# A gated recurrence followed by a max-out layer: copies that either VectorE or ScalarE may do, and a new order of all queues

## Chip, cores and metric

The kernel runs on one NeuronCore of a Trainium2 chip. The metric is the device time of one execution in microseconds. TensorE is called PE here, VectorE DVE, ScalarE ACT, GpSimd POOL and SyncE SP. Each engine works through its own queue of instructions strictly in the order in which they were written; semaphores make an instruction wait for another engine or for a transfer.

## The reference

```python
# q, k, v, f_logit: (B=4, H=8, S=768, D=48), float32
f = 1 / (1 + exp(-f_logit))
for t in range(S):
    state = f[:, :, t, :, None] * state + einsum('bhd,bhe->bhde', k[:, :, t], v[:, :, t])
    y[:, :, t] = einsum('bhd,bhde->bhe', q[:, :, t], state)

x = y.transpose(0, 2, 1, 3).reshape(B * S, H * D)      # 3072 x 384
h1, h2 = x @ w1, x @ w2                                # 384 x 1024 each
out = maximum(h1, h2) @ w_out                          # 1024 x 384
```

## The kernel before

The sequence is cut into windows of 256 positions, three for each of the four batch entries: twelve stages s = 0 to 11, where stage s is window s // 4 of batch entry s % 4. A partition of the 128 holds two neighbouring positions. Each window consists of two halves h = 0 and 1 of 128 positions, and the state is carried from half to half and, by way of stage s - 4, from window to window.

The kernel writes max(h1, h2) as relu(h1 - h2) + h2. So it needs two matrices made from the weights: `wd` = w1 - w2, and `m2` = w2 @ w_out. The output is xT·m2 + relu(xT·wd)·wo.

What each engine does is written as a list of short words, `ORDER`, and the kernel issues the steps in the order of that list. Since every step writes instructions into several queues, the list fixes the order of all five queues. No scheduler moves anything later. The words are these, with the stage behind the letter:

- `Lf`, `Lk`, `Lq`, `Lv`: load an input of a stage (384 KB) from SP's queue. f has 3 buffers, k and q have 4, v has 6, and a load waits until its buffer is free. It also waits for an earlier transfer, as the transfers of the SP and ACT queues share eight completion semaphores. `W1:i`, `W2:i`: gather 128 rows of a weight (512 KB) from POOL's queue. `Wo:i`: load half of `w_out` from SP's queue.
- `E`: two activations on ACT (exp, then ln) that give -log f in `both`. `e` on POOL or `g` on DVE adds the two positions into `es`.
- `C`: five matmuls on PE for the running sum `cum`; DVE makes `even`. `X`: five exponentials on ACT (`f_inv`, `f_dec`, `f_last`).
- `K` on POOL or `k` on DVE: `kp` = k times `f_inv`. `Q` or `q`: `qp` = q times `f_dec`, likewise. `V` on DVE or `U` on ACT: v in bf16 (`vb`).
- `T`: 32 transposes of `kp` and `qp` on PE (line 236), and two copies of the results, `trs`, on DVE (line 239).
- `A`: the products of keys and queries, 32 matmuls, and four products with a mask on DVE (`at_m`, line 264).
- `D` and `N`: what the window adds to the state (32 matmuls, or 16 where one half is enough), and the new state for half 0 and half 1. Where there is an older state, DVE adds (line 336) and POOL multiplies (line 337).
- `S`: the state's part of y. `Z`: a tiny ACT copy of it. `Y`: the rest of y on PE (line 306), two ACT copies into `xT` (line 344), and two small transfers from ACT's queue that close gaps in `xT` (line 347).
- `d<s>.<i>`: a quarter of relu(xT·wd): six matmuls (line 360) and a relu on ACT (line 362). `o<s>.<i>`: half of the output of stage s: eleven matmuls (lines 370 and 373), a copy on DVE (line 375), and with the second half the store from SP's queue.
- `wc`, `wT`, `wo`, `wm`, `ws`: casts, transposes and products of the weights. The letter behind names the engine that does the cast or copy: a for ACT, v for DVE, p for POOL. `ws` makes half of `wd` (line 405), `wm` a third of `m2` (line 399).

All matrix results go through eight PSUM banks that are handed out in turn, so a new one waits for the reader of the eighth one before.

Of the kernel before, what the change touches and what calls it, by code (L numbers as in the profile page):

```python
# [14 lines left out]


ORDER = """
Lf:0 E0 Lv:0 e0 C0 X0 Lk:0 V0 W2:0 Lf:1 K0 Lq:0 Lv:1 E1 q0 e1 T0 Lk:1 C1 Lf:2 W1:0 Lq:1 A0 X1 wca0
V1 D0 S0 K1 W1:1 W2:1 W2:2 E2 Lf:3 N0 g2 W1:2 Lk:2 Lq:2 q1 D1 Z0 Y0 T1 N1 E3 e3 A1 wTa0 C2 S1 Lv:2
wcp1 C3 Wo:0 Z1 wcv2 Wo:1 Lf:4 X2 wsv0 wsv1 Y1 q2 X3 k2 Lk:3 wTa1 Lv:3 Lq:3 V2 wTv2 d0.0 d0.1 d0.2  # L20
d0.3 Lf:5 T2 wov0 d1.0 d1.1 wov2 Lk:4 d1.2 woa3 A2 Lv:4 D2 d1.3 Lq:4 Lf:6 wop1 E4 wma2 Lk:5 wma0 N2
g4 Q3 k3 wmv1 C4 U3 S2 D3 Z2 N3 Lq:5 X4 o1.0 T3 E5 Y2 e5 o0.0 K4 C5 X5 A3 Lf:7 V4 S3 Q4 o0.1 T4 Z3
Lv:5 E6 Y3 Lf:8 D4 Lq:6 e6 Lk:6 N4 Lv:6 d2.0 o1.1 A4 K5 E7 S4 Z4 d2.1 Lq:7 d2.2 d2.3 Lf:9 Y4 V5 D5
Lv:7 N5 d3.0 d3.1 g7 d3.2 C6 q5 Lf:10 o2.0 X6 K6 Lv:8 C7 X7 T5 o2.1 A5 S5 Lk:7 E8 Z5 e8 d3.3 U6 d4.0
d4.1 C8 Y5 q6 q7 X8 Lk:8 K7 V7 o3.0 Lq:8 T6 d4.2 o3.1 d4.3 E9 E10 D6 e9 N6 A6 d5.0 o4.0 Lv:9 d5.1
d5.2 d5.3 C9 e10 D7 N7 S6 Z6 Lf:11 X9 Lq:9 Lk:9 Lq:10 T7 Y6 Q8 o4.1 U9 Lk:10 A7 K8 V8 S7 o5.0 C10 Z7
k9 E11 Lv:10 Y7 Lv:11 Lq:11 X10 D8 Q9 Lk:11 T8 o5.1 d6.0 d6.1 d6.2 A8 S8 Q10 D9 Z8 d6.3 d7.0 T9 Y8
o6.0 d7.1 K10 d7.2 A9 e11 T10 U10 d7.3 o6.1 C11 o7.0 X11 S9 Z9 D10 K11 A10 Y9 o7.1 d8.0 d8.1 d8.2
V11 Q11 d8.3 S10 T11 Z10 D11 Y10 o8.0 d9.0 o8.1 d9.1 d9.2 d9.3 A11 S11 d10.0 Z11 d10.1 d10.2 Y11
o9.0 d10.3 o9.1 o10.0 d11.0 d11.1 d11.2 d11.3 o10.1 o11.0 o11.1  # L30
"""


# [1 line left out]
def kernel(  # L35
# [20 lines left out]
    nc = tc.nc  # L56
    B, H, S, D = q.shape
# [20 lines left out]
    def bank(name, dtype=F32):  # L78
        return psum.tile([C, 2048 // (4 if dtype == F32 else 2)], dtype, name=name, tag="bank")
# [47 lines left out]
    for nm, n_bufs in (("es", 2), ("kp", 3), ("qp", 2), ("vb", 3)):  # L127
        padded[nm] = []
        for i in range(n_bufs):
            t = consts.tile([C, H, DP] if nm == "es" else [C, 2, H, DP], BF16, name=f"{nm}{i}")  # L130
# [3 lines left out]
    def pad(nm, s):  # L134
        return padded[nm][s % len(padded[nm])]
# [86 lines left out]
    def stage_V(s, copy):  # L222
        copy(pad("vb", s)[:, :, :, 0:D], by_parity(loaded[s]["v"]))

    def stage_T(s):
        t = work.tile([C, 2, 2, NP, 2, HC], BF16, name="trs", tag="trs", bufs=3)
        ps = [bank(f"trp{h}", BF16).rearrange("p (x j a t) -> p x j a t", x=2, j=NP, a=2)
              for h in range(2)]
        for x, nm in enumerate(("kp", "qp")):
            src = pad(nm, s)  # L230
            for j in range(NP):
                for par in range(2):
                    for h in range(2):
                        rows = slice(h * HC, (h + 1) * HC)
                        pair = src[rows, par, 2 * j:2 * j + 2, :].rearrange("p r d -> p (r d)")
                        nc.tensor.transpose(out=ps[h][:, x, j, par, :], in_=pair,  # L236
                                            identity=ident[rows, rows])
        for h in range(2):
            nc.vector.tensor_copy(t[:, h], ps[h])  # L239
        tr[s] = t  # L240

    def stage_A(s):
        t = tr[s]
        m = work.tile([C, 2, NP, 2, C], BF16, name="at_m", tag="at_m")
        for jj in range(2):
            ps = [bank(f"at{r}").rearrange("p (j a t) -> p j a t", j=2, a=2) for r in range(2)]
            for j in range(2 * jj, 2 * jj + 2):
                for par in range(2):
                    for h in range(2):
                        for r in range(2):  # L250
                            rows = slice(r * DP, r * DP + D)
                            nc.tensor.matmul(out=ps[r][h * HC:(h + 1) * HC, j % 2, par, :],  # L252
                                                  lhsT=t[rows, h, 0, j, par, :],
                                                  rhs=t[rows, h, 1, j].rearrange("p a t -> p (a t)"),
                                                  start=True, stop=True, skip_group_check=True)
            at[s, jj] = ps
        at[s] = m

    def stage_A_dve(s):
        m = at[s]  # L260
        for jj in range(2):
            ps = at.pop((s, jj))
            for r in range(2):
                nc.vector.tensor_mul(m[:, r, 2 * jj:2 * jj + 2], ps[r],  # L264
                                     mask.rearrange("p j a b t -> p j a (b t)"))

    ys = {}

    def has_state(s, h):
        return s >= B or h > 0  # L270

    def state_before(s, h):
        return states[s][:, 0] if h else states[s - B][:, 1]
# [22 lines left out]
    def stage_Yv(s):  # L296


        m, vb = at.pop(s), pad("vb", s)
        for j in range(NP):  # L300
            for par in range(2):
                for r in range(2):
                    for h in (1, 0):
                        rows = slice(h * HC, (h + 1) * HC)
                        first = j == 0 and par == 0 and not has_state(s, h)
                        nc.tensor.matmul(  # L306
                            out=ys[s][h][r * DP:(r + 1) * DP, j, :], lhsT=vb[rows, par, 2 * j + r, :],
                            rhs=m[rows, r, j, par, :], start=first,
                            stop=(j == NP - 1 and par == 1), skip_group_check=True)

    def stage_D(s):
        kp, vb = pad("kp", s), pad("vb", s)
        halves = range(2) if s < n_s - B else range(1)
        sadd[s] = [bank(f"sadd{h}")[:, 0:NP * DP].rearrange("p (j e) -> p j e", j=NP) for h in halves]
        for j in range(NP):
            for par in range(2):
                for r in range(2):
                    for h in halves:
                        rows = slice(h * HC, (h + 1) * HC)
                        nc.tensor.matmul(  # L320
                            out=sadd[s][h][r * DP:(r + 1) * DP, j, :], lhsT=kp[rows, par, 2 * j + r, :],
                            rhs=vb[rows, par, 2 * j + r, :], start=(j == 0 and par == 0),
                            stop=(j == NP - 1 and par == 1), skip_group_check=True)
        states[s] = work.tile([C, 2, NP, DP], BF16, name="state", tag=f"state{s % B}")

    def stage_D_dve(s, h):
        if h >= len(sadd[s]):
            return
        ps = sadd[s][h]
        f_last = dec[s][2][:, :, h:h + 1].to_broadcast([C, NP, DP])  # L330
        new = states[s][:, h]
        if not has_state(s, h):
            nc.vector.tensor_mul(new, ps, f_last)  # L333
        else:
            tmp = work.tile([C, NP, DP], F32, name="tmp_s", tag="tmp_s")
            nc.vector.tensor_add(tmp, ps, state_before(s, h))  # L336
            nc.gpsimd.tensor_mul(new, tmp, f_last)  # L337

    xT, gT, obs = {}, {}, {}

    def stage_Y_act(s):
        x = xpool.tile([C, NP, 2, 2, HC], BF16, name="xT", tag="xT", bufs=3)
        for h, ps in enumerate(ys.pop(s)):
            nc.scalar.copy(x[:, :, :, h, :], ps.rearrange("p j (a t) -> p j a t", a=2))  # L344
        x = x.rearrange("p j a h t -> p j (a h t)")
        for r in range(2):
            nc.scalar.dma_start(out=x[r * DP + D:(r + 1) * DP, 0:KT, :],
                                in_=x[r * DP:r * DP + D, KT, :])
        xT[s] = x
        tr.pop(s)  # L350
# [59 lines left out]
    def attention(fn):  # L410
        return lambda a: fn(int(a))
# [4 lines left out]
    def rows_of(dst, w):  # L416
# [8 lines left out]
        "K": lambda a: stage_M(int(a), "k", nc.gpsimd), "k": lambda a: stage_M(int(a), "k", nc.vector),  # L425
        "Q": lambda a: stage_M(int(a), "q", nc.gpsimd), "q": lambda a: stage_M(int(a), "q", nc.vector),
        "V": lambda a: stage_V(int(a), nc.vector.tensor_copy), "U": lambda a: stage_V(int(a), nc.scalar.copy),
        "T": attention(stage_T), "S": attention(stage_S), "Z": attention(stage_Z),
        "A": lambda a: (stage_A(int(a)), stage_A_dve(int(a))),
        "Y": lambda a: (stage_Yv(int(a)), stage_Y_act(int(a))),  # L430
        "D": lambda a: (stage_D(int(a)), stage_D_dve(int(a), 0)),
        "N": lambda a: stage_D_dve(int(a), 1),
        "d": lambda a: piece_d(*map(int, a.split("."))), "o": lambda a: piece_o(*map(int, a.split("."))),
# [37 lines left out]
```

## Time and profile before

| what | us |
|---|---|
| median of 5 runs | 148.35 |
| lowest and highest of them | 147.28 and 149.04 |
| the profiled execution | 148.52 |
| its span, first to last instruction | 146.8 |
| PE busy | 124.2 (85%) |
| DVE busy | 95.9 (65%) |
| ACT busy | 89.8 (61%) |
| POOL busy | 59.3 (40%) |

In a profile, busy time and shares are averages over the span. The rows of digits cut the span into 40 equal slices of 3.67 us; a digit is the busy share of a slice in tenths. A group of instructions has its line, engine, operation, output and input tiles, count, busy time and mean. The chain of work that ended last goes back from the last instruction, at each step to what released it; each of its lines has a start, a length, and what ran. In the timeline an instruction's wait stands in brackets, with what ended it. Matmuls overlap, so a matmul's own length is longer than what it costs the queue; the distances in the chain are the better measure.

### The profile page before, as it was taken

The page shows a single profiled execution, that of the slowest core. Times are in us where ns is not written, and L with a number is a line of the kernel's source. Part 1 is how long each engine was busy: PE and PEld are TensorE (multiplying, and loading weights), DVE is VectorE, ACT ScalarE, POOL GpSimd, SP SyncE. Part 2 cuts the span into 40 slices and gives each one's busy share as a digit, 9 for nine tenths or more (in the row PEclk, how much of TensorE's full clock was granted, in tenths as well). Part 3 has the DMA queues.
Part 4 walks back from the last instruction along what each step waited for, and adds up shares of the span by engine and source line. Part 5 has one row for each costly group of instructions (what it writes and reads, how often), then busy time and mean ns, then how long its engine had stood idle before and what let it go on. Part 6 is the DMA issues. An engine that isn't in the chain of part 4 may idle for free.

```text
span 146.8 us, 5288 instructions
## 1 busy us (share of the span) xinstructions
PE 124.2 (85%) x2292; PEld 91.1 (62%) x2292; DVE 95.9 (65%) x179; ACT 89.8 (61%) x179; POOL 59.3 (40%) x68
## 2 busy tenths in 40 slices
PE   0017378769999999999997999999999999999990
PEld 0005266546866667876865786786767877866750
DVE  5157988489698697877893858958497752613030
ACT  3462947774697886959967886596527634650500
POOL 7376776232019484544214639195404610000000
PEclk9999999999999999999999999999999999999999
DMA  4999999999989706999997985993002300202022
GB/s 104 323 304 330 300 296 378 386 375 258 279 212 272 201 13 187 308 253 277 294 345 204 274 215 186 241 305 125 22 0 112 121 4 33 92 13 107 4 107 107
DMA packets 55128, 29.25 MB, mean 199 GB/s; under 512 B 50624, under 2 KB 52800, under 8 KB 55104
## 3 DMA queue, kind: packets, MB, share of 16 engines
q1 hardware_dynamic: 52704, 25.17, 59.6%
q0 software_dynamic: 864, 3.15, 6.1%
q10 hardware_dynamic: 1536, 0.59, 1.5%
q8 instruction: 18, 0.29, 0.8%
q14 instruction: 6, 0.05, 0.1%
HBM read 23.59 MB, written 4.72 MB: 193 GB/s over the span
## 4 chain that ended last, share of the span: by engine, by line
PE 62%; DMA 15%; POOL 7%; DVE 6%; ACT 5%; issue 2%; ACTq 0%; SPq 0%; DVEq 0%
PE h L360 23%; PE o L373 17%; PE o L370 7%; DMA ft<-in_f_logit_dram 6%; DMA w_f<-in_moe_w_dram,row_of 5%; DMA xT<-xT 4%; PE trp L236 4%; PE y L306 3%; PE at L252 3%; PE y L286 3%; POOL kp L219 2%; POOL w_f L102 2%; PE sadd L320 2%; DVE qp L219 1%; POOL qp L219 1%
## 5 line engine op out<-in xcount | busy, mean ns | idle before, releaser
L362 ACT ACTIVATE gT<-h 128x512 bf16<-128x512 f32 x48 | 28.1, 599 | 22.9 <-PE h L360 20.7
L360 PE MATMUL h<-xT,wd 128*128 128x256 bf16 x288 | 37.6, 285 | 2.2 <-DVE wd L405 1.4
L373 PE MATMUL o<-wo,gT 128*128 128x384 bf16 x192 | 35.1, 326 | 0.0
L360 PEld LDWEIGHTS <-wd 128*128 128x128 bf16 x288 | 28.3, 102 | 8.5 <-DVE wd L405 1.7
L264 DVE TENSOR_TENSOR at_m<-at,mask 128x512 bf16<-128x512 f32 x48 | 29.7, 682 | 5.3 <-PE at L252 5.3
L375 DVE COPY ob<-o 128x384 f32<-128x384 f32 x24 | 13.3, 555 | 21.8 <-PE o L373 21.8
L373 PEld LDWEIGHTS <-gT 128*128 128x128 bf16 x192 | 18.8, 98 | 12.4
L337 POOL TENSOR_TENSOR state<-tmp_s,f_last 128x256 bf16<-128x256 f32 x16 | 10.5, 657 | 36.0 <-DVE tmp_s L336 24.8
L219 POOL TENSOR_TENSOR kp<-kt,f_inv 128x768 bf16<-128x768 f32 x9 | 16.3, 1815 | 8.9 <-ACT f_inv L211 4.6
L239 DVE COPY trs<-trp 128x1024 bf16<-128x1024 bf16 x24 | 15.4, 683 | 3.7 <-PE trp L236 3.6
L370 PE MATMUL o<-m,xT 128*128 128x384 bf16 x72 | 15.7, 328 | 0.0
L344 ACT CAST xT<-y 128x512 bf16<-128x512 f32 x24 | 12.9, 591 | 3.9 <-PE y L306 3.9
L210 ACT ACTIVATE f_inv<-cum 128x384 f32<-128x384 f32 x12 | 5.9, 496 | 13.9 <-DVE even L201 9.8
L180 ACT ACTIVATE both<-ft 128x768 f32<-128x768 f32 x12 | 10.2, 851 | 3.9 <-DMA ft<-in_f_logit_dram 2.3
L187 POOL TENSOR_TENSOR es<-both 128x384 bf16<-128x384 f32 x9 | 9.0, 997 | 8.9 <-issue 5.3
L219 POOL TENSOR_TENSOR qp<-qt,f_dec 128x768 bf16<-128x768 f32 x6 | 11.6, 1940 | 0.0
L195 PE MATMUL cum<-es,u_inc 128*128 128x384 bf16 x12 | 4.6, 380 | 7.8 <-POOL es L187 7.8
L201 DVE TENSOR_TENSOR even<-cum,both 128x384 f32<-128x384 f32 x12 | 6.6, 551 | 6.6 <-PE cum L197 5.9
L181 ACT ACTIVATE both<-both 128x768 f32<-128x768 f32 x12 | 10.1, 844 | 0.4
L252 PE MATMUL at<-trs 48*64 48x128 bf16 x384 | 9.2, 234 | 1.3 <-DVE trs L239 1.3
L336 DVE TENSOR_TENSOR tmp_s<-sadd,state 128x256 f32<-128x256 f32 x16 | 6.7, 421 | 4.8 <-POOL state L337 2.9
L286 PE MATMUL y<-trs,state 48*64 48x128 bf16 x160 | 7.1, 227 | 2.6 <-DVE state L333 2.6
(64 smaller groups left out, 156.9 us busy)
## 6 DMA issues: line engine op xcount, KB each, us to landing
ft<-in_f_logit_dram SPq DMA_DIRECT2D x12, 384.0 KB, 5.8
vt<-in_v_dram SPq DMA_DIRECT2D x12, 384.0 KB, 5.3
kt<-in_k_dram SPq DMA_DIRECT2D x12, 384.0 KB, 6.4
qt<-in_q_dram SPq DMA_DIRECT2D x12, 384.0 KB, 6.1
out_dram<-ob SPq DMA_DIRECT2D x12, 384.0 KB, 2.5
wo_f<-in_moe_w_out_dram SPq DMA_DIRECT2D x2, 768.0 KB, 11.2
xT<-xT ACTq DMA_DIRECT2D x24, 24.0 KB, 3.5
w_f<-in_moe_w_dram,row_of POOLq DMA_INDIRECT x6, 6.6
```

Of the source, the lines that this page charges most:

```text
L219: engine.tensor_mul(pad(nm + "p", s)[:, :, :, 0:D], by_parity(loaded[s][nm]), t.rearrange("p two (h d) -> p two h d", h=H))
L239: nc.vector.tensor_copy(t[:, h], ps[h])
L252: nc.tensor.matmul(out=ps[r][h * HC:(h + 1) * HC, j % 2, par, :], lhsT=t[rows, h, 0, j, par, :], rhs=t[rows, h, 1, j].rearrange("p a t -> ...
L264: nc.vector.tensor_mul(m[:, r, 2 * jj:2 * jj + 2], ps[r], mask.rearrange("p j a b t -> p j a (b t)"))
L286: nc.tensor.matmul(out=ys[s][h][r * DP:(r + 1) * DP, j, :], lhsT=st[rows, j, :], rhs=t[rows, h, 1, j].rearrange("p a t -> p (a t)"), start ...
L337: nc.gpsimd.tensor_mul(new, tmp, f_last)
L344: nc.scalar.copy(x[:, :, :, h, :], ps.rearrange("p j (a t) -> p j a t", a=2))
L360: nc.tensor.matmul(out=ps[:, f, :], lhsT=wd[:, kt, ff * C:(ff + 1) * C], rhs=xT[g][:, kt, :], start=(kt == 0), stop=(kt == KT - 1))
L362: nc.scalar.activation(gT[g][:, 2 * fp:2 * fp + 2, :], ps, AF.Relu)
L370: nc.tensor.matmul(out=ps, lhsT=xT[g][:, kt, cols], rhs=m2[:, kt, :], start=(kt == 0), stop=False)
L373: nc.tensor.matmul(out=ps, lhsT=gT[g][:, ff, cols], rhs=wo[:, ff, :], start=False, stop=(ff == FG - 1))
L375: nc.vector.tensor_copy(obs[g][:, par, :], ps)
```

## The change

There are two parts. First, two new words. `t` is a `T` whose second copy goes to ACT instead of DVE; `y` is a `Y` whose second copy into `xT` goes to DVE instead of ACT. Five of the twelve stages use `t` (0, 3, 6, 9, 10) and six use `y` (1, 2, 3, 4, 8, 11). Second, the whole list is written anew, so the order of every queue and the choice of engine for many steps differ. The order came from a table of the costs of each step, in which transfers in flight together now share the DMA engines packet by packet.

```diff
 ORDER = """
-Lf:0 E0 Lv:0 e0 C0 X0 Lk:0 V0 W2:0 Lf:1 K0 Lq:0 Lv:1 E1 q0 e1 T0 Lk:1 C1 Lf:2 W1:0 Lq:1 A0 X1 wca0
-V1 D0 S0 K1 W1:1 W2:1 W2:2 E2 Lf:3 N0 g2 W1:2 Lk:2 Lq:2 q1 D1 Z0 Y0 T1 N1 E3 e3 A1 wTa0 C2 S1 Lv:2
-wcp1 C3 Wo:0 Z1 wcv2 Wo:1 Lf:4 X2 wsv0 wsv1 Y1 q2 X3 k2 Lk:3 wTa1 Lv:3 Lq:3 V2 wTv2 d0.0 d0.1 d0.2
-d0.3 Lf:5 T2 wov0 d1.0 d1.1 wov2 Lk:4 d1.2 woa3 A2 Lv:4 D2 d1.3 Lq:4 Lf:6 wop1 E4 wma2 Lk:5 wma0 N2
-g4 Q3 k3 wmv1 C4 U3 S2 D3 Z2 N3 Lq:5 X4 o1.0 T3 E5 Y2 e5 o0.0 K4 C5 X5 A3 Lf:7 V4 S3 Q4 o0.1 T4 Z3
-Lv:5 E6 Y3 Lf:8 D4 Lq:6 e6 Lk:6 N4 Lv:6 d2.0 o1.1 A4 K5 E7 S4 Z4 d2.1 Lq:7 d2.2 d2.3 Lf:9 Y4 V5 D5
+Lf:0 Lk:0 E0 g0 Lq:0 Lf:1 Lv:0 C0 V0 Lk:1 E1 Lf:2 Lv:1 Lq:1 e1 X0 k0 q0 E2 C1 W2:0 Lf:3 W1:0 t0 V1
+Lq:2 D0 e2 C2 X1 W2:1 k1 X2 Lk:2 W2:2 wca0 Q1 Lf:4 Wo:1 W1:1 A0 N0 T1 S0 E3 Z0 D1 W1:2 g3 Q2 Wo:0 N1
+wca1 Y0 A1 wTv0 S1 Z1 K2 wca2 C3 y1 wop3 X3 wsv0 Lv:2 wsv1 wop2 wTv1 Lk:3 wTv2 T2 E4 wov1 d0.0 Lf:5
+e4 d0.1 d0.2 Lq:3 K3 d0.3 d1.0 Q3 V2 wov0 d1.1 d1.2 Lk:4 d1.3 A2 E5 D2 wmv0 C4 Lf:6 Lv:3 e5 wmv1 N2
+wmv2 t3 Lq:4 Lf:7 X4 S2 Z2 E6 C5 Lv:4 y2 A3 o1.0 X5 Lq:5 Lk:5 K4 Lf:8 g6 Lv:5 V3 o1.1 U4 Q4 o0.0
+Lq:6 C6 T4 D3 E7 Q5 Lv:6 Lk:6 D4 o0.1 X6 S3 Z3 Lv:7 Lq:7 Lk:7 K5 N4 N3 U5 d2.0 y3 A4 d2.1 S4 Z4 d2.2
+Lf:9 e7 Lq:8 d2.3 V6 y4 D5 T5 C7 Lf:10 o2.0 K6 E8 X7 Lk:8 N5 o2.1 d3.0 d3.1 e8 Q7 q6 Lf:11 Lv:8 A5
+D6 t6 E9 d3.2 d3.3 d4.0 K7 d4.1 N6 d4.2 C8 X8 o3.0 A6 k8 S5 g9 Z5 S6 Z6 Y5 o3.1 Lq:9 Lk:9 d4.3 Lv:9
+Lk:10 Y6 E10 Lq:10 Lk:11 T7 Q8 T8 o4.0 d5.0 V8 C9 g10 X9 V7 o4.1 K9 d5.1 A7 E11 D8 D7 C10 d5.2 d5.3
...
+d8.2 d8.3 D11 S10 T11 Z10 Y10 o8.0 o8.1 d9.0 d9.1 A11 S11 Z11 d9.2 d9.3 d10.0 y11 o9.0 o9.1 d10.1
+d10.2 d10.3 d11.0 d11.1 o10.0 d11.2 d11.3 o10.1 o11.0 o11.1
 """
...
-    def stage_T(s):
+    def stage_T(s, copy=nc.vector.tensor_copy):
...
-        for h in range(2):
-            nc.vector.tensor_copy(t[:, h], ps[h])
+        nc.vector.tensor_copy(t[:, 0], ps[0])
+        copy(t[:, 1], ps[1])
...
-    def stage_Y_act(s):
+    def stage_Y_act(s, copy=nc.scalar.copy):
...
-        for h, ps in enumerate(ys.pop(s)):
-            nc.scalar.copy(x[:, :, :, h, :], ps.rearrange("p j (a t) -> p j a t", a=2))
+        for h, (ps, fn) in enumerate(zip(ys.pop(s), (nc.scalar.copy, copy))):
+            fn(x[:, :, :, h, :], ps.rearrange("p j (a t) -> p j a t", a=2))
...
+        "t": lambda a: stage_T(int(a), nc.scalar.copy),
+        "y": lambda a: (stage_Yv(int(a)), stage_Y_act(int(a), nc.vector.tensor_copy)),
```

More of the change, by code (lines that the diff above doesn't have):

```diff
@@ L23 @@
-Lv:5 E6 Y3 Lf:8 D4 Lq:6 e6 Lk:6 N4 Lv:6 d2.0 o1.1 A4 K5 E7 S4 Z4 d2.1 Lq:7 d2.2 d2.3 Lf:9 Y4 V5 D5
[L24 to L27, printed above, removed]
@@ L28 @@
-o6.0 d7.1 K10 d7.2 A9 e11 T10 U10 d7.3 o6.1 C11 o7.0 X11 S9 Z9 D10 K11 A10 Y9 o7.1 d8.0 d8.1 d8.2
-V11 Q11 d8.3 S10 T11 Z10 D11 Y10 o8.0 d9.0 o8.1 d9.1 d9.2 d9.3 A11 S11 d10.0 Z11 d10.1 d10.2 Y11
-o9.0 d10.3 o9.1 o10.0 d11.0 d11.1 d11.2 d11.3 o10.1 o11.0 o11.1
+Lf:0 Lk:0 E0 g0 Lq:0 Lf:1 Lv:0 C0 V0 Lk:1 E1 Lf:2 Lv:1 Lq:1 e1 X0 k0 q0 E2 C1 W2:0 Lf:3 W1:0 t0 V1
+Lq:2 D0 e2 C2 X1 W2:1 k1 X2 Lk:2 W2:2 wca0 Q1 Lf:4 Wo:1 W1:1 A0 N0 T1 S0 E3 Z0 D1 W1:2 g3 Q2 Wo:0 N1
+wca1 Y0 A1 wTv0 S1 Z1 K2 wca2 C3 y1 wop3 X3 wsv0 Lv:2 wsv1 wop2 wTv1 Lk:3 wTv2 T2 E4 wov1 d0.0 Lf:5
@@ L31 @@
+Lk:10 Y6 E10 Lq:10 Lk:11 T7 Q8 T8 o4.0 d5.0 V8 C9 g10 X9 V7 o4.1 K9 d5.1 A7 E11 D8 D7 C10 d5.2 d5.3
+d6.0 X10 Q9 N7 d6.1 e11 d6.2 o5.0 A8 S7 Z7 S8 Z8 K10 Y7 o5.1 Q10 d6.3 V9 Lv:10 Lv:11 y8 Lq:11 t9 t10
+U10 o6.0 C11 o6.1 X11 d7.0 d7.1 d7.2 D9 A9 V11 d7.3 d8.0 d8.1 k11 S9 D10 A10 q11 Z9 Y9 o7.0 o7.1
+d8.2 d8.3 D11 S10 T11 Z10 Y10 o8.0 o8.1 d9.0 d9.1 A11 S11 Z11 d9.2 d9.3 d10.0 y11 o9.0 o9.1 d10.1
+d10.2 d10.3 d11.0 d11.1 o10.0 d11.2 d11.3 o10.1 o11.0 o11.1
 """
@@ L427 @@
         "V": lambda a: stage_V(int(a), nc.vector.tensor_copy), "U": lambda a: stage_V(int(a), nc.scalar.copy),
-        "T": attention(stage_T), "S": attention(stage_S), "Z": attention(stage_Z),
+        "T": attention(stage_T), "t": lambda a: stage_T(int(a), nc.scalar.copy),
+        "S": attention(stage_S), "Z": attention(stage_Z),
         "A": lambda a: (stage_A(int(a)), stage_A_dve(int(a))),
         "Y": lambda a: (stage_Yv(int(a)), stage_Y_act(int(a))),
+        "y": lambda a: (stage_Yv(int(a)), stage_Y_act(int(a), nc.vector.tensor_copy)),
         "D": lambda a: (stage_D(int(a)), stage_D_dve(int(a), 0)),
```

## Prediction

> **What bounds the kernel now.** I read the page first: its 40 slices, queues and groups. Then the chain of work that ended last, in order of time, the timeline of the first 36 us, and each DMA's time to landing.
>
> ```profile
> span 146.8 us, 5288 instructions
> ...
> PE   0017378769999999999997999999999999999990
> ...
> DVE  5157988489698697877893858958497752613030
> ACT  3462947774697886959967886596527634650500
> ...
> DMA  4999999999989706999997985993002300202022
> ```
>
> PE is full from slice 11 (37 us) to 143 us. Before that the DMA row is full and PE is not: the span is a start bound by transfers and dependences, then about 106 us bound by PE.
>
> ```profile
> 29.81 1.77 DVE wd L405
> 31.58 0.05 issue
> 31.63 5.30 PE h L360 x24
> 36.93 0.65 PE trp L236 x32
> ...
> 134.91 2.62 PE h L360 x24
> ```
>
> In the chain the first dense work, d0.0, starts at 31.63 once `wd` exists. Its first 24 matmuls take 5.30 us; the same 24 take 2.62 us at the end, so PE ran at half rate until about 37 us.
>
> At full rate the chain gives per step: C 0.24, T 0.57, A 0.57, Y 0.57, S 0.45, D 0.39 (0.24 with one half), d 0.65, o 1.79, wm 1.3 us. Adding these between markers, PE lost about 1.0 us between A2 (39.6) and Y4 (61.3), 0.5 before Y5 (72.5), 1.0 before d5.0 (80.5) and 0.5 up to A8 (97.6). Then nothing. The middle holds 3 us to win, the start more.
>
> ```profile
> 7.35 1.17 POOL L102 DMA_INDIRECT w_f<-in_moe_w_dram,row_of  x1 [0.19 <-POOL es L187]
> ...
> 22.02 0.98 POOL L102 DMA_INDIRECT w_f<-in_moe_w_dram,row_of  x1 [0.16 <-issue]
> ...
> 24.53 1.01 ACT L390 COPY w2T<-w2t 128x1024 bf16<-128x1024 bf16 x1
> ```
> ```profile
> 74.95 5.42 DMA xT<-xT
> 80.37 0.14 issue
> 80.50 0.81 PE h L360 x6
> ```
> ```profile
> q1 hardware_dynamic: 52704, 25.17, 59.6%
> q0 software_dynamic: 864, 3.15, 6.1%
> ```
>
> The last of six gathers (W1:2) is issued at 22.02 and lands 7.7 us later; it makes `wd`. The wait at 80.5 is an xT copy behind three loads. Gather packets average 3.15 MB / 864 = 3.6 KB, load packets 25.17 MB / 52704 = 0.48 KB.
>
> **What the Trainium skill says.** "DMA: Bandwidth & Descriptors", section "Queues, rings and completion order": each DMA engine goes round between queues packet by packet. With packets seven times larger a gather should crowd out loads. The trace agrees: the k load issued at 6.75, as the first gather starts, takes 8.4 us to land against 3.5 for the first load. "TensorE: Matmul & The Clock Gate", section "Part 1: The HAM clock gate": PE starts at half clock and warms after about 3.4 us of sustained work; the 5.30 against 2.62 us agrees. "SBUF — State Buffer", section "Who interferes with whom": GpSimd and a VectorE operation with two SBUF inputs exclude each other. The trace agrees: the product `qp` on DVE takes 1.88 us at 10.19, beside POOL's `kp`, and 0.95 us at 19.45.
>
> **The change, part by part.** PE's work is the same 2292 matmuls; only their order changes.
>
> *Shared evacuations.* Five of twelve steps T (t0, t3, t6, t9, t10) send one copy from DVE (0.64 us, half of 1.29) to ACT (1.0, from the row of `w2T` on ACT). Six Y (y1, y2, y3, y4, y8, y11) send one copy from ACT (0.59) to DVE. DVE has no such row: below, 0.56 (the `ob` copy, fewer elements), above, 0.68 (`at_m`, same elements with a mask); I take 0.60, as nothing makes it a second reader. ACT: +5.0 - 3.5 = +1.5 us; DVE: +3.6 - 3.2 = +0.4 us. Over the span this is nothing, and `xT` is ready about 0.5 us sooner for these six, under other PE work.
>
> *Other engine choices.* es goes from 9 POOL and 3 DVE to 7 and 5 (POOL 1.0, DVE 0.56); k from 9 and 3 to 8 and 4; q from 6 and 6 to 9 and 3 (POOL 1.9, DVE about 1). POOL gains 3 x 1.9 - 1.8 - 2.0 = 2 us of 59; it is not the bound. The weight casts `w2b` all go to ACT, all `m2` copies to DVE.
>
> *The start, walked by hand in the new queues.* Loads run one per 1.2 us (4.34, 5.55, 6.73, 7.97).
> - ACT has E1 before X0. f1 is now the fourth load: 7.97. E1 8.0-9.7, X0 9.7-11.6 (was 8.46-10.2). es0 on DVE saves 0.4, but X0 waits for E1. kp0 and qp0 both on DVE: 12.6. T0 ends about 13.3 (was 12.8).
> - POOL: es1 until 10.8, then W2:0 at 10.8 and W1:0 at 12.1; E2 ends 13.4, es2 14.4; W2:1 14.5, W2:2 15.7, Q1 16.9-18.7, W1:1 18.7, the state product, W1:2 at 20.4 (was 22.02).
> - PE is in order, and C2 (es2) now stands before A0: A0 at 15.2 (was 14.1). DVE has even2 and kp1 ahead of `at_m`: 16.8-19.3 (was 14.8-17.3). Y0 ends 21.4, A1 22.5 (was 23.5).
> - A gather's data flow some 2.5 to 3 us after its issue, and take 1.6 us each (0.52 MB at 320 GB/s). The pairs flow about 13.6-17 and 17-20.2. The ninth load (q1) lands at about 16.5, the tenth (f3), caught by the second pair, about 20.9, q2 25.3, k2 26.5.
> - E3 is before xT0 on ACT (it was after): 20.9-22.6. Then two weight casts and xT0 to 25.0 (was 21.2), its copies issued 25.1-26.3. At 28.87 such a copy took 4.9 to 5.1 us: landing at 30.8.
> - es3 on DVE waits for E3, with `at_m` of A1 behind it: 23.6-26.1. y1 ends 27.2; its DVE copy stands ahead of `wd`: 27.3-27.9, then `wd` 29.7 and 31.4. W1:2 itself lands about 26.5 and no longer decides.
> - T2 now precedes d0.0: Q2 25.3-27.1, K2 to 29.6, T2 30.4.
>
> So d0.0 starts at the latest of 29.7, 30.4 and 30.8, call it 30.9, against 31.63: 0.7 us. T2, 0.65 us of the chain, is already done. PE waits little from 20 us on, so I take it warm 0.3 to 0.4 us sooner: together 1.7 us at the first wm step (39.4, was 41.10). The four wo casts would be done by 35 to 37 us; no wait.
>
> *The middle.* From A2 to y4 the PE sum is 20.3 us, the DVE instructions from `at_m` of A2 through `at_m` of A4 sum to 19.9, and ACT's (its 0.6 us DMA issues included) to 20.6. Three in-order engines are full at once. Before, the stretch lost 1.0; I take 1.5 now: -0.5 us against the change. Behind a late DVE copy there stand the mask products, then Y, then d.
> Later, for d5.0, PE has ahead of it Y5, o3.1, d4.3, Y6, T7, T8, o4.0 = 7 us, about as much as before, but the load queue now has its f11 and v8 well before and q9, k9 after Y5. I take the 1.0 us wait at 80.5 as gone. Every later d has 5.5 to 10 us of PE work after its Y, against 3.7 us from Y11 to landing at 132.5: covered. The shortest A-to-Y distances (A4, A11: 2.4 us) equal those of before.
>
> *The end.* After y11 PE has 15.3 us of work, after Y11 before 14. The last o, copy and output are the same: 3.9 us.
>
> Sum: 1.7 - 0.5 + 1.0 = 2.2 us. The profiled execution took 148.52 us, of which 146.8 is span; 148.52 - 2.2 = 146.3. The median of the five runs is 148.35, 0.17 less than the profiled one; I leave that inside the range.
>
> **The rivals.**
> *A. More is won.* If the gathers, spread over 10 us instead of four in 4.5, leave f3 its share and xT0 lands by 28, d0.0 follows at about 29.7, and PE, kept busy by y1, wT and T2 from 26, is warm 1.5 us earlier: 148.5 - 4.5 = 144.0. For it: W1:2 is earlier. Against it: xT0 is behind E3.
> *B. The lead is eaten.* PE arrives at 39.4, but at_m of A4 decides, DVE being at 19.9 of 20.3 us, and 1.7 to 2 us are lost by y4: 148.4. For it: DVE and ACT slices of 8 and 9 there already. Against it: ACT loses four halves of Y in exactly this part.
> *C. Slower: gathers crowd out f3.* Place: E3 ahead of both xT0 (ACT) and `at_m` of A1 (DVE). If f3 lands at 24.5 instead of 20.9, E3 ends 26.2, xT0's copies are issued at 28.7 and land near 34.5: d0.0 is 3 us later than before, less 0.65 for T2 and 0.4 elsewhere: 150.5. It decides from f3 at about 22.5 on; each us after that is a us of span. For it: two pairs of gathers in a row, and the 8.4 us load. Against it: f3 is only tenth in its queue.
> *D. The choice of engine for the evacuations alone* would move nothing: 1.5 us of ACT work in 147 us. It is part of the forecast, not a case.
>
> **How the numbers follow.** Forecast 0.46 (its own range 144.9 to 147.6), A 0.10, B 0.15, C 0.29. A measurement here tells about 1% from no change, so the limits are 146.9 and 149.8. The forecast lies about three quarters below 146.9 (0.34), the rest within; A is faster; B within; C slower. Faster 0.44, same 0.27, slower 0.29. The range takes half of A, all of B and most of C: 143.9 to 150.8.
>
> **What would show it.** Right: f3 landing near 21 us, W1:2 issued near 20.4, d0.0 near 31 with xT0 as its last wait, T2 ahead of it, the first wm step near 39.4, y4 before 61, no wait of PE on an xT copy near 80. Wrong: d0.0 after 32, or PE idle between A2 and y4 on `at_m`; a late start for another reason than f3 or xT0 would make the walk wrong even if the time fits.

## Result: 1.5% less was forecast, and less than 1% of difference was measured

| | before | after |
|---|---|---|
| median of all executions, us | 148.43 (79) | 148.71 (42) |
| lowest and highest, us | 147.16 and 150.35 | 146.43 and 151.98 |
| profiled execution, us | 148.52 | 148.53 |
| its span, us | 146.8 | 146.8 |

The ratio after to before is 0.9966, with a 95% interval of 0.9943 to 0.9989. (Like every ratio here it leaves out executions more than 1.5% above the fastest of their kernel, of which the changed kernel has more; so it lies below 1 while the medians stand the other way round.) Either way this is within 1%, where 146.3 us had been forecast. The two spans agree to the tenth. What lies inside them does not.

The rows of the changed kernel, each digit a slice of 3.67 us:

```profile
span 146.8 us, 5296 instructions
...
PE   0105566749995899999999999999999999999990
...
DVE  5349989389996678886949798478469753730130
ACT  3489955476836687659697489943994333607300
...
DMA  4999999999999519929997499606930122002022
```

Up to 33 us PE's row is, taken as a whole, less full than before (34 tenths in the first nine slices, against 39). The thirteenth slice (44 to 48 us) shows a 5 where before there was a 9. The next has an 8, and from there on PE is full.

The chain of work that ended last, for the start and for that slice:

```profile
21.51 8.33 DMA w_f<-in_moe_w_dram,row_of
...
29.96 4.51 DVE wd L405 x2
...
34.52 5.04 PE h L360 x36
...
40.40 1.41 PE m2p L399 x8
...
44.67 0.62 PE trp L236 x32
...
45.31 0.02 ACT trs L239
...
46.22 0.50 ACT f_inv L210
...
47.99 0.06 ACT seen L294
...
48.09 0.64 PE y L306 x32
```

Two things are to be seen. Up to 40.40 (the first wm step) `wd` still decides, by way of the last gather, W1:2. That step came at 41.10 before, so the new order leads by 0.7 us here. Then, between 45 and 48 us, the chain runs through ACT: a copy of transposes (`trs`, line 239), the five exponentials of X4 (the first is shown), and the copy `seen` of Z2, for which the matrix products of y2 wait.

The timeline of ACT in the changed kernel around it (start, length, what ran, and in brackets the idle time ahead of it with its releaser):

```profile
40.95 0.84 ACT L181 ACTIVATE both<-both 128x768 f32<-128x768 f32 x1
45.31 1.01 ACT L239 COPY trs<-trp 128x1024 bf16<-128x1024 bf16 x1 [3.52 <-PE trp L236]
46.22 0.50 ACT L210 ACTIVATE f_inv<-cum 128x384 f32<-128x384 f32 x1
...
47.85 0.18 ACT L294 COPY seen<-y 128x4 f32<-128x4 f32 x1
```

and that of PE:

```profile
45.69 0.24 PE L197 MATMUL cum<-ones,es 128*128 128x2 bf16 x4
48.09 0.64 PE L306 MATMUL y<-at_m,vb 64*64 64x128 bf16 x32 [2.15 <-ACT seen L294]
```

On DVE, X4's last input, `even` of stage 4, is made from 43.17 to 43.71:

```profile
43.17 0.54 DVE L201 TENSOR_TENSOR even<-cum,both 128x384 f32<-128x384 f32 x1
```

So ACT is idle for 3.5 us, in the later part of which X4 is ready behind the copy. ACT can't go on because t3's second copy, now its own, heads its queue and waits for PE's transposes. So X4 runs after the copy instead of ahead of it, Z2 after X4, and y2 after Z2, since Z2 reads the PSUM bank that y2 writes next. PE loses 2.15 us.

To see what the loss did to the lead, I added up PE's steps at their full-rate cost in both traces and compared at equal clock times how much had been done: after leads before by 0.8 us at 40 us, trails it by 1.5 at 48 us, by 1.1 at 80, by 0.6 at 92, and by 0.1 at 104. By the same sums PE loses 3.2 us between 48 and 104 us before and 1.5 after. Single places over half a microsecond are only the wait before d5.0 (0.9, before, the xT copy at 80.5) and S6 (0.65 up to 78.7, after, which ends on a `seen` once more); the rest are tenths at many steps. From 104 us on the two are alike.

So the zero is, in the profiled executions, a lead of 0.7 us, a loss of 2.2 from one moved copy, and some 1.5 won back later.

### The profile page after: what moved, and what is told of

Read it like the earlier page. It is cut to its first block, busy times and chain, and to the rows that moved or that the text cites. A ratio compares the mean times of both kernels' runs of the same rounds, so it can differ in the third digit from the quotient of the medians.

```text
span 146.8 us, 5296 instructions
## 1 busy us (share of the span) xinstructions
PE 120.9 (82%) x2292; PEld 89.5 (61%) x2292; DVE 98.9 (67%) x184; ACT 89.4 (61%) x174; POOL 61.5 (42%) x68
## 4 chain that ended last, share of the span: by engine, by line
PE 59%; DMA 13%; ACT 7%; POOL 7%; DVE 6%; issue 3%; SPq 2%; ACTq 1%; POOLq 0%; DVEq 0%
PE o L373 19%; PE h L360 18%; PE o L370 8%; DMA w_f<-in_moe_w_dram,row_of 6%; DMA ft<-in_f_logit_dram 4%; POOL w_f L102 4%; DMA vt<-in_v_dram 3%; PE y L306 3%; DVE wd L405 3%; PE m2p L399 3%; PE trp L236 3%; PE at L252 2%; ACT gT L362 2%; SPq L93 2%; PE y L286 2%
## 5 line engine op out<-in xcount | busy, mean ns | idle before, releaser
L360 PE MATMUL h<-xT,wd 128*128 128x256 bf16 x288 | 36.0, 280 | 2.5 <-DVE wd L405 2.3
L219 POOL TENSOR_TENSOR qp<-qt,f_dec 128x768 bf16<-128x768 f32 x9 | 17.2, 1910 | 5.6 <-issue 2.9
L219 POOL TENSOR_TENSOR kp<-kt,f_inv 128x768 bf16<-128x768 f32 x8 | 14.5, 1816 | 9.7 <-ACT f_inv L211 9.7
L306 PE MATMUL y<-at_m,vb 64*64 64x128 bf16 x384 | 8.6, 234 | 4.8 <-ACT seen L294 4.8
L344 ACT CAST xT<-y 128x512 bf16<-128x512 f32 x18 | 9.9, 586 | 3.2 <-PE y L306 3.2
L187 POOL TENSOR_TENSOR es<-both 128x384 bf16<-128x384 f32 x7 | 7.5, 1068 | 9.3 <-DVE vb L223 5.6
L306 PEld LDWEIGHTS <-vb 64*64 64x64 bf16 x384 | 7.1, 116 | 6.1 <-issue 6.0
L238 DVE COPY trs<-trp 128x1024 bf16<-128x1024 bf16 x12 | 8.1, 683 | 2.3 <-PE trp L236 2.3
L197 PEld LDWEIGHTS <-es 128*128 128x128 bf16 x48 | 3.1, 102 | 10.6 <-issue 9.8
L223 DVE CAST vb<-vt 128x768 bf16<-128x768 f32 x9 | 8.0, 885 | 1.3 <-DMA vt<-in_v_dram 1.3
```

Source lines behind the costliest of these rows:

```text
L219: engine.tensor_mul(pad(nm + "p", s)[:, :, :, 0:D], by_parity(loaded[s][nm]), t.rearrange("p two (h d) -> p two h d", h=H))
L306: nc.tensor.matmul(out=ys[s][h][r * DP:(r + 1) * DP, j, :], lhsT=vb[rows, par, 2 * j + r, :], rhs=m[rows, r, j, par, :], start=first, stop ...
L344: fn(x[:, :, :, h, :], ps.rearrange("p j (a t) -> p j a t", a=2))
L360: nc.tensor.matmul(out=ps[:, f, :], lhsT=wd[:, kt, ff * C:(ff + 1) * C], rhs=xT[g][:, kt, :], start=(kt == 0), stop=(kt == KT - 1))
```

## The experiments

In their expectations the letters stand for theories. Z: the changed kernel is held at y2 by Z2, which waits in ACT's queue behind X4 and t3's copy. The others are named where they come up. Ratios are to the kernel before, with 95% intervals; medians in us.

### Z2 first

```diff
-wmv2 t3 Lq:4 Lf:7 X4 S2 Z2 E6 C5 Lv:4 y2 A3
+wmv2 t3 Lq:4 Lf:7 S2 Z2 X4 E6 C5 Lv:4 y2 A3
```

> The changed kernel with one word moved: Z2 before the five exponentials X4 on ScalarE (they stood the other way round). Theory Z (y2 waits 2.3 us at 45.8 because its release, the tiny copy Z2, stands in ScalarE's queue behind X4, and X4 behind t3's copy): Z2 runs at about 46.3, right after t3's copy; y2 starts near 46.4 instead of 48.1, the wait shrinks from 2.3 to about 0.7 us, and the time falls by 1.2 to 1.7 us against the changed kernel (ratio to the kernel before about 0.985 to 0.990). Rival F (VectorE and ScalarE are full in this stretch, the lead goes anyway): y2 starts earlier but the time is lost again before y4, total unchanged within 0.4 us (ratio about 0.997).

Measured: 146.76, ratio 0.9907 (0.9879 to 0.9935). Its timeline on ACT and on PE:

```profile
45.95 1.01 ACT L239 COPY trs<-trp 128x1024 bf16<-128x1024 bf16 x1 [3.52 <-PE trp L236]
46.86 0.17 ACT L294 COPY seen<-y 128x4 f32<-128x4 f32 x1
```
```profile
47.08 0.64 PE L306 MATMUL y<-at_m,vb 64*64 64x128 bf16 x32 [0.51 <-ACT seen L294]
```

The exponentials no longer stand between t3's copy and Z2, and the wait at y2 falls from 2.15 to 0.51 us. Nothing but the order of Z2 and X4 in ACT's queue differs, and the kernel is 0.6% nearer to the forecast by the ratios. That is about 0.9 us, less than the 1.2 to 1.7 expected. Theory Z holds in its mechanism. The 3.52 us of idle ACT ahead of the copy are still there.

### T3 instead of t3

```diff
-wmv2 t3 Lq:4
+wmv2 T3 Lq:4
```

> The changed kernel with T3 in place of t3: both copies of the transposes of stage 3 on VectorE again. Theory Z: X4 no longer stands behind a copy that waits for T3; it runs from 43.8 as soon as its input is there, Z2 at about 45.7, y2 at about 45.8; the wait of 2.3 us goes wholly, against 0.6 us later start of A3: 1.5 to 2.2 us less than the changed kernel (ratio about 0.982 to 0.988). Rival F: VectorE, given 0.64 us more, is late with the mask products of A3 and A4; time unchanged or up to 0.6 us more (ratio 0.997 to 1.001).

Measured: 145.76, ratio 0.9858 (0.9815 to 0.9902). ACT's timeline:

```profile
43.44 0.49 ACT L210 ACTIVATE f_inv<-cum 128x384 f32<-128x384 f32 x1 [2.13 <-DVE even L201]
...
45.14 0.16 ACT L294 COPY seen<-y 128x4 f32<-128x4 f32 x1
```

and PE's:

```profile
45.37 0.64 PE L306 MATMUL y<-at_m,vb 64*64 64x128 bf16 x32
```

With that one copy back on DVE, X4 starts as soon as its input is there, 2.8 us earlier than in the changed kernel. Z2 is done before y2 needs it, and y2 starts at 45.37 without a wait. The profiled execution is ahead of the changed kernel's by 0.5 us at the first wm step, by 2.4 at o1.0 behind y2, and by 2.9 at the end, so most of the difference arises here. One copy of 1 us on an engine that is 61% busy was worth about 1.1% of the time of the kernel (0.9966 against 0.9858).

### The new order with the old copies

Every `t` is written `T` and every `y` is written `Y`, in the new order.

> The new order with every t written T and every y written Y, so all copies on the engines they had before; the order of the words is that of the changed kernel. If the shared copies are worth nothing by themselves (as predicted, +-0.4 us in all) but t3 does harm by theory Z: the wait at y2 goes, while six Y copies return to ScalarE, which costs up to 1 us elsewhere: 0.5 to 2 us below the changed kernel. If the shared copies are what makes the new order work (rival): 1 to 3 us slower than the changed kernel.

Measured: 145.76, ratio 0.9836 (0.9801 to 0.9870). The order alone brings 1.6%. The other ten shared copies are worth nothing that can be measured: with them and T3 the ratio was 0.9858, and the intervals overlap.

### The old order with the new copies

The two words are added to the kernel before, with `t` and `y` for the same stages as in the change.

> The order before with t at stages 0, 3, 6, 9, 10 and y at stages 1, 2, 3, 4, 8, 11: the shared copies alone, in an order that was not made for them. Prediction: the copies alone move nothing (ratio 0.997 to 1.003). Rival: a copy placed on an engine whose next instruction waits for something else holds that engine up, as t3 does in the new order; then 0.5 to 2 us slower (ratio 1.003 to 1.014).

Measured: 152.7, ratio 1.0314 (1.0261 to 1.0367): slower, as the rival in the expectation had it, by more than twice what it allowed. DVE's timeline shows where y1's second copy stands:

```profile
30.38 4.03 DVE L405 TENSOR_TENSOR wd<-w_f 128x1536 bf16<-128x1536 f32 x2 [1.10 <-DMA w_f<-in_moe_w_dram,row_of]
34.33 0.68 DVE L344 CAST xT<-y 128x512 bf16<-128x512 f32 x1
```

ACT's, what waits for it:

```profile
27.45 0.60 ACT L344 CAST xT<-y 128x512 bf16<-128x512 f32 x1
35.09 1.21 ACTq L347 DMA_DIRECT2D xT<-xT  x2
36.35 0.49 ACT L210 ACTIVATE f_inv<-cum 128x384 f32<-128x384 f32 x1 [8.30 <-DVE qp L219]
```

and PE's, d0 and the start of d1:

```profile
32.79 5.30 PE L360 MATMUL h<-xT,wd 128*128 128x256 bf16 x24 [2.42 <-DVE wd L405]
...
39.98 2.12 PE L360 MATMUL h<-xT,wd 128*128 128x256 bf16 x18 [1.03 <-DMA xT<-xT]
```

In this order `wsv0` and `wsv1` stand ahead of y1, so the copy is behind 4 us of `wd`. ACT issues the transfers of `xT` for both halves, so it stands at them for 7 us, with X3 behind. The same words that cost nothing in the new order (but for t3) cost 3.1% in the old. A word's price depends on what is ahead of it in the queue it joins, and on what joins behind it.

### The old order with the new copies, but Y1

```diff
-wcp1 C3 Wo:0 Z1 wcv2 Wo:1 Lf:4 X2 wsv0 wsv1 y1 q2
+wcp1 C3 Wo:0 Z1 wcv2 Wo:1 Lf:4 X2 wsv0 wsv1 Y1 q2
```

> The old order with the new copies, but Y1 in place of y1. In the run with y1, its VectorE copy stood behind wd, ScalarE's queue waited 7.0 us (28.0 to 35.1) before it could issue the transfers of xT 1, and d1.0 came late. Theory Q (a copy moved to another engine holds up both queues): the 1.4 us wait before d1.0 goes, ScalarE's X2 starts near 30 again, and the ratio falls from 1.031 to 1.010 to 1.022, what is left being t3, y2 and y4. Rival: the 3% come from the sum of the moved work; then Y1 takes off less than 0.5%.

Measured: 149.44, ratio 1.0137 (1.0073 to 1.0201), within the range expected: writing Y1 takes off 1.8% of the 3.1%. (What the expectation calls X2 is X3; it starts at 32.46, not near 30.) PE no longer waits before d1.0. But that wait is not all that sets the two profiled executions apart. At the first wm step they lie 3.4 us apart: 0.8 us is an earlier d0.0, 1.0 the wait for `xT`, and most of the rest PE's rate. With y1 the 24 matmuls of d0 took 5.30 us, as in the kernel before; here they took 1.48 us for each twelve. Whether y1 has to do with that rate is not shown, so how much of the 1.8% is the copy's own wait stays open.

Two other waits of PE remain, in both kernels (the lines are of this one):

```profile
51.38 0.32 PE L195 MATMUL cum<-es,u_inc 128*128 128x384 bf16 x1 [1.41 <-POOL es L187]
...
63.81 0.45 PE L320 MATMUL sadd<-vb,kp 64*64 64x64 bf16 x32 [1.40 <-DVE vb L223]
```

The first is C5: it needs `es` of stage 5, made from E5, which stands behind t3's copy on ACT. The second is D5: `vb` of stage 5 stands behind y4's copy on DVE.

### Transfers of w_out later

The first half of the forecast's loss is at the start: W1:2 was to land at 26.5 and did at 29.84. One explanation was the 1.5 MB of `w_out` that share the engines with the gathers; by its rival, L in the expectation, moving them brings nothing. This kernel has T3, loads `w_out` after v2 and k3, and gives POOL's two casts of it to ACT.

```diff
-... Lf:4 Wo:1 W1:1 A0 ... g3 Q2 Wo:0 N1 ... y1 wop3 X3 wsv0 Lv:2 wsv1 wop2 wTv1 Lk:3 wTv2 T2 ... d0.0 ... d0.1
+... Lf:4 W1:1 A0 ... g3 Q2 N1 ... y1 X3 wsv0 Lv:2 wsv1 wTv1 Lk:3 Wo:1 Wo:0 wTv2 T2 ... d0.0 ... d0.1 woa3 woa2
```

> The changed kernel with T3 for t3, and in it the two loads of w_out issued after v2 and k3 instead of after f4; the casts of their second half done on ScalarE between d0.1 and d0.2 instead of on GpSimd. Theory P (the last gather took 8.3 us to land in the changed kernel, against 5 to 6 in the prediction's walk, because all the bytes of f4 and w_out were in flight beside it): W1:2 lands at about 28 instead of 29.8, wd starts there, d0.0 starts near 30 instead of 31.8, and 1 to 1.8 us are won against the kernel with T3 alone (ratio 0.973 to 0.979). Rival L (the gather's landing is set by the other gathers and its own issue): W1:2 still lands at 29.5 to 30, d0.0 moves by less than 0.4 us, and the total by less than 0.5 us.

Measured: 145.74, ratio 0.9845 (0.9799 to 0.9891), the time of T3 alone. W1:2 was issued at 22.05 and landed at 29.31, 7.3 us later, where after has 8.3: the bytes of `w_out` are about 1 us of it at most, half of which a later issue takes back, and the total shows nothing of it. The landing is 0.2 us earlier than L had it; on d0.0 (31.57, against 31.84 with T3 alone) and on the total L is right.

### Casts off POOL

T3, and `wop3` and `wop2` become `woa3` and `woa2` behind d0.1, with the loads where they were.

> The changed kernel with T3 for t3, and with the two casts of w_out that GpSimd does beside wd moved to ScalarE, between d0.1 and d0.2. The two instructions of wd took 4.16 us beside those casts against 3.5 in the kernel before. If GpSimd's casts hold VectorE up, wd takes 3.4 to 3.5 us; d0.0 starts 0.1 to 0.3 us earlier, and the total changes by 0 to 0.5 us against the kernel with T3 alone, since the second half of wd is not what PE waits for there (ratio 0.982 to 0.986). If they do not, wd stays at 4.2 and the total too.

Measured: 147.19, ratio 0.9884 (0.9849 to 0.9919), with single executions from 145.07 to 148.89; 0.982 to 0.986 had been expected. The interval overlaps that of T3 alone. The mechanism is there: the two halves of `wd` take 4.57 us together in the changed kernel, where POOL's casts of `wo` run from 29.73 to 32.85, and 3.51 us without them. In the group of `wd` on DVE (lowest, median and highest length in ns), in the changed kernel:

```profile
L405 DVE TENSOR_TENSOR wd<-w_f x2: 2201/2286/2372, 30.0 to 32.1; 128x1536 bf16<-128x1536 f32 x2
```

and here:

```profile
L405 DVE TENSOR_TENSOR wd<-w_f x2: 1751/1755/1759, 31.1 to 32.8; 128x1536 bf16<-128x1536 f32 x2
```

But the microsecond does not arrive in the total. In this execution `es` of stage 3 on DVE took 2.89 us,

```profile
L187 DVE TENSOR_TENSOR es<-both x1: 2889/2889/2889, 22.8 to 22.8; 128x384 bf16<-128x384 f32 x1
```

where in the kernel with T3 alone it took

```profile
L187 DVE TENSOR_TENSOR es<-both x1: 548/548/548, 21.8 to 21.8; 128x384 bf16<-128x384 f32 x1
```

By the profile it begins before POOL's Q2 in both, 0.64 us ahead in the former and 0.69 in the latter, and in the former it ends 0.4 us after Q2 (23.47 to 25.30). The Trainium skill, "SBUF — State Buffer", section "Who interferes with whom", says that VectorE and GpSimd share one pair of SBUF ports as an exclusive lock, and the lengths agree: 0.55 against 2.89 us. That the choice of which comes first varies from one execution to the next, and spreads the times, would be an explanation, but it is not shown. What the record shows is that the spread goes with the clock granted to PE: the twelve executions with a mean of 0.999 or 1.000 took 145.07 to 147.25 us, the ten with 0.988 took 147.85 to 148.89. And with the transfers of `w_out` later, `es` took 2.87 us in the profiled execution, and the time was still that of T3 alone.

### PE kept busy

The last kernel, with T2's transposes written three times over.

```diff
-        for x, nm in enumerate(("kp", "qp")):
+        for x, nm in [(0, "kp"), (1, "qp")] * (3 if s == 2 else 1):
```

> As the kernel with the casts moved to ScalarE, and the 32 transposes of stage 2 done three times over (64 transposes of no use, into the same banks before they are read), so that PE is busy in the 2 us before d0.0. Theory H (PE drops to half rate because of the wait before d0.0, and runs d0.0 to d0.2 at 1.28 us each instead of 0.65): PE runs at full rate when d0.0 starts near 31.8 or within 0.5 us of it; the d pieces end 1.0 to 1.7 us sooner; total 0.8 to 1.5 us below the kernel with casts moved alone (ratio 0.973 to 0.979). Rival: the rate does not follow from what PE does just before, or d0.2 and d1.0 wait for wd and xT instead: less than 0.4 us.

Measured: 147.67, ratio 0.9962 (0.9934 to 0.9991): missed. PE's timeline:

```profile
30.50 0.61 PE L236 MATMUL trp<-ident,qp 64*128 64x64 bf16 x16
30.93 0.48 PE L236 MATMUL trp<-ident,kp 64*128 64x64 bf16 x16
31.25 0.40 PE L236 MATMUL trp<-ident,qp 64*128 64x64 bf16 x16
...
32.04 5.67 PE L360 MATMUL h<-xT,wd 128*128 128x256 bf16 x48
...
39.64 0.45 PE L320 MATMUL sadd<-vb,kp 64*64 64x64 bf16 x32 [1.37 <-DVE vb L223]
```

and DVE's:

```profile
37.43 2.16 DVE L223 CAST vb<-vt 128x768 bf16<-128x768 f32 x1
```

PE has its full rate when d0.0 starts: 48 matmuls of d0 and d1 take 5.67 us here and 7.22 with T3 alone. That the repeated transposes brought this about, as theory H has it, is not shown. They begin at 30.93, and already from about 31.1 the rate is up (0.61 us for sixteen, then 0.48, then 0.40). In the kernel with the transfers of `w_out` later, which repeats nothing, the first 24 matmuls of d0 take 3.32 us, where before they took 5.30.

The Trainium skill, "TensorE: Matmul & The Clock Gate", section "Part 1: The HAM clock gate", says that activity releases the throttle. The changed kernel's trace agrees. These are stretches of 3.4 us (the last of 3.6), with PE's busy time and, in the column behind the count, the clock granted:

```profile
22.80:26.20 3.40, 1.45 (x29) 1.00 1.09 403
26.20:29.60 3.40, 2.92 (x52) 0.50 1.04 396
29.60:33.00 3.40, 1.37 (x40) 1.00 1.05 294
33.00:36.40 3.40, 3.10 (x16) 0.51 0.98 252
36.40:40.00 3.60, 3.60 (x69) 0.99 1.14 310
```

Each half-rate stretch follows one in which PE worked for less than half the time, and the two full ones behind them follow 2.9 us of work or more. (Ahead of the first recorded change of clock, which is at 37 us in the kernel before, the views show 1.00; there the rate has to be read from the matmuls' lengths.) So, as far as these traces show it, d0's rate depends on where such a stretch ends as well as on what PE did in it.

What was won on d0 was lost at once. D2 needs `vb` of stage 2, and the cast of 0.55 us takes 2.16 beside POOL's Q3; the first wm step comes at 40.12, against 39.84 with T3 alone. A start made faster on PE arrives at DVE's queue. That explains why nothing was gained, but not why the time is above T3 alone, by 1.5 us in the ratios: the profiled execution loses that later, with 1.31 us in T5 for which the profile names no cause. That stays open.

### es of stage 3 on POOL

T3, and `g3` becomes `e3`, so that the order against Q2 is fixed.

> The changed kernel with T3 for t3, and in it es of stage 3 made on GpSimd (between the last gather and Q2) instead of on VectorE. In the profiles so far that VectorE sum took 0.55 us where it began before GpSimd's Q2, and 2.8 to 2.9 us where it began after it (in the three kernels whose profiles were slower early). Theory G (the two engines' products of two SBUF inputs exclude each other, and which comes first is chance): with both on GpSimd the order is fixed, at_m of A1 starts at 22.3 to 23 in every run; the time is that of T3 alone, 145.5 to 146 us, with a spread under 1 us and no runs of 147 to 148. Rival (the slower early start comes from late transfers): spread and median as in the kernels with casts moved, 145 to 148.5.

Measured: 146.78 (146.39 to 147.58), ratio 0.9895 (0.9857 to 0.9932). The spread is 1.2 us, near what theory G said, but the time had been expected to be that of T3 alone and lies 1 us above it (0.5 by the ratios, whose intervals overlap). `at_m` of A1 starts at 23.3, against 22.6 with T3 alone. So the theory is not confirmed by the time, and what spreads the times of the other kernels stays open.

### All of these at once

The kernel with PE kept busy, with `e3` for `g3` and `vb` of stage 2 on ACT (`U2` for `V2`).

> All that helped together: T3 for t3, es of stage 3 on GpSimd, the casts of w_out on ScalarE, the transposes of stage 2 done three times over to keep PE busy (64 of no use), and v of stage 2 cast on ScalarE (it took 2.2 us on VectorE beside GpSimd's Q3, and D2 waited 1.4 us for it where PE was kept busy). Theory: d pieces end near 37.6 as in the run with PE kept busy, D2 follows without a wait, and 1.0 to 1.5 us are won over T3 alone: 144.3 to 144.9 us (ratio 0.973 to 0.979). Rival: the casts of w_out, whose loads land at 32, or VectorE behind them, hold up the first wm step as before; then 145.5 to 146.

Measured: 145.82, ratio 0.9827 (0.9782 to 0.9871), where 0.973 to 0.979 had been expected. D2's wait is gone, and the first wm step comes at 38.83, 1.0 us ahead of T3 alone. That lead is gone by 63 us; most of it goes at y4, where PE waits 0.85 us for a `seen` once more. In the total the kernel can't be told from the new order with the old copies. DVE shows what is late now:

```profile
30.22 3.43 DVE L405 TENSOR_TENSOR wd<-w_f 128x1536 bf16<-128x1536 f32 x2 [2.60 <-DMA w_f<-in_moe_w_dram,row_of]
```

DVE idles 2.6 us for W1:2, issued at 21.51 and landed at 30.09.

### The last gathers earlier

The same, with Q1 on DVE (`q1`), so that POOL is free to issue W1:1 and W1:2 directly after W2:2. Theory I: the landing follows the issue.

```diff
-k1 X2 Lk:2 W2:2 wca0 Q1 Lf:4 Wo:1 W1:1 A0 N0 T1 S0 E3 Z0 D1 W1:2 e3 Q2
+k1 q1 X2 Lk:2 W2:2 W1:1 W1:2 wca0 Lf:4 Wo:1 A0 N0 T1 S0 E3 Z0 D1 e3 Q2
```

> As the kernel with all fixes, and the last two gathers W1:1 and W1:2 issued directly after W2:2, ahead of qp of stage 1, which moves from GpSimd to VectorE. In all runs of the new order so far W1:2 was issued at 21.5 to 22.5 and landed at 29.3 to 30.1, and wd waited for it. Theory I (the landing follows the issue): issued at about 19, it lands at 27 to 27.7; wd starts when xT and A1's products let it, near 27.6; d0.0 then waits for xT 0 (about 30.5) instead, 1 to 1.5 us earlier than before, and the total is 144.3 to 145 us. Rival B (the landing is set by the bytes in flight): it still lands at 29 or later, d0.0 stays at 31.5 to 32 and the total at 145.5 to 146.

Measured: 146.04 (144.75 to 149.25), ratio 0.9813 (0.9757 to 0.9869). W1:2 is issued at 19.60 and lands at 27.69, 2.4 us earlier for an issue 1.9 us earlier, so theory I holds for the landing. DVE then works on `wd` without that wait, from 27.95:

```profile
27.95 3.44 DVE L405 TENSOR_TENSOR wd<-w_f 128x1536 bf16<-128x1536 f32 x2
```

d0.0 starts at 31.13, directly after the last of the repeated transposes. The lead over T3 alone is 1.5 us at the first wm step and gone by 63 us; most of it goes in A4 and T5, where PE waits 0.73 and 0.76 us and the profile names no cause. Whether this is faster in total, the intervals don't tell.

### The best version

The new order with the old copies, the gathers early, `q1`, and `e3`; no repeated transposes.

> The new order with every copy on its old engine, and in it the same two gathers early, qp of stage 1 on VectorE and es of stage 3 on GpSimd; nothing else changed, no useless transposes. Theory I: d0.0 near 30.5, 1 us ahead of the kernel with the old copies alone (145.76): 144.5 to 145.2 us. Rival B: 145.5 to 146.5.

Measured: 144.35, ratio 0.9713 (0.9655 to 0.9771). It beats the kernel before by 2.9% and the changed one by 2.5% (0.9713 to 0.9966). Its executions lie between 143.23 and 148.38, two of the seven above 146. The profiled one is the 148.38: POOL's Q2 waited 4.1 us for its load there, and d0.0 started at 34.80. So no trace shows that d0.0 starts near 30.5 in the others, which would make theory I the cause of the gain; that, and why the load came late, stays open.

## Why the prediction was wrong, point by point

**The step that failed: "The middle".** Three sums near 20 us (PE, DVE, ACT) were taken as the danger, and 0.5 us was put down. Distances from A to Y and from Y to d were called covered. Left out was a third thing that Y waits for: Z, called "a tiny ACT copy", and what stands ahead of it in ACT's queue. It cost 2.15 us at y2. Z2 first takes most of that wait away, T3 all of it, and the time falls with it. The same term was missing at y1, where Z1 stands behind ACT's issue of the transfers of xT 0:

```profile
26.68 1.06 PE L306 MATMUL y<-at_m,vb 64*64 64x128 bf16 x32 [2.34 <-ACT seen L294]
```

There it did not decide, as `wd` came later still. Rival B had the right outcome, but its mechanism (`at_m` of A4 behind a full DVE) did not occur: in the changed kernel's waits the only one of PE put down to `at_m` is 0.2 us, and DVE was itself idle for 2.2 us, until y2 was done.

**The step behind it: "Over the span this is nothing".** The price of the shared copies was taken from the sum of each engine's work (+1.5 and +0.4 us). For ten of the eleven in the new order that is right. The eleventh, t3, had nearly all of the effect, and in the old order the same eleven cost 3.1%. What decides is which instruction waits behind the copy while it is itself waiting. Case D, that the choice of engine "alone would move nothing", was folded into the forecast on the same ground and is wrong.

**The start: right in kind, 1 us too much.** The walk held to within about 0.5 us up to A1: `kp` and `qp` done at 12.3 (forecast 12.6), A0 at 15.3 (15.2), `at_m` from 16.83 (16.8), the end of Y0 near 21.9 (21.4). xT 0 landed at 30.9 (30.8), and T2 stood ahead of d0.0, from 29.5. Two terms were mis-sized. W1:2 was issued at 21.51 instead of 20.4 and took 8.3 us instead of 6, so it landed at 29.84 and still decided. And `wd` took 4.5 us in all instead of 3.5, since POOL's casts of `wo` now run beside it. d0.0 started at 32.22 instead of 30.9, later than before (31.63); the lead of 0.7 at the first wm step, where 1.7 had been forecast, comes from T2 already done and from PE's rate. PE had its full rate 0.6 us sooner than before (36.5 instead of 37.1), and for its first matmuls of d0 as well. The forecast had 0.3 to 0.4 for this, on the ground that PE waits little from 20 us on; it waited 2.34 us at y1 and 2.03 at d0.0, so the agreement here is luck.

**The load of f3: wrong, with no harm.** It landed at 15.1, not 20.9: it took 4.9 us, as the loads ahead of it did, though it was issued 0.6 us before the first gather, like the load of 8.4 us before the change that the prediction took as agreement. Longer were only the loads from the eleventh on (6.8 and 10.9 us for the next two), which did not decide; that the gathers were the reason is not shown. So rival C, given 0.29, had no place to happen.

**Right, in part by luck.** The order alone was worth 1.6% (2.4 us; the forecast for the whole was 2.2). Its parts differ, though: by the same sums as above, the new order with the old copies leads by 1.4 us at 40 us, 0.7 at 64 and 2.7 at 104, where the forecast had 1.7, 1.2 and 2.2. The wait on an xT copy at 80.5 is gone, though S6 now loses 0.65 us nearby. The end is the same.

## What to carry to other kernels

A copy given to another engine is priced by its place in that engine's in-order queue: when its input comes, and what stands behind it that was ready before. The sum of work on both engines says nothing of this. List for every step all it waits for, with the small readers of a PSUM bank that it will write again, and follow each back to the head of its queue. When an order and a set of choices change together, run each alone: here a sum near zero hid a gain of 1.6% and a loss of 1.3%.

## What the runs showed that was not expected

- The last gather of 512 KB (W1:2) landed 7.3 to 8.6 us after its issue at 19.6 to 22.5 us (19.60 to 27.69, 21.51 to 30.09, 22.05 to 29.31). Moving the loads of `w_out` away left 7.3. Why so long stays open.
- Beside POOL, DVE was slower not only with two inputs, as the prediction has it (the addition `es` took 2.89 us instead of 0.55, a half of `wd` 2.37 instead of 1.75), but with one as well: the cast of `vb` took 2.16 us instead of 0.55.
- DVE copies the half of y into `xT` in 0.69 us, ACT in 0.59; the half of the transposes takes DVE 0.68 and ACT 1.01.
